# Causal mask as a matmul, and the copies of keys and queries spread anew over the engines

## The chip, the cores and the metric

One core of one Trainium2 chip runs the whole kernel as one program. The metric is device time in microseconds (us) of one execution; lower is better. The engines are named as the profile names them: PE (TensorE, matmuls; PEld is its weight load), DVE (VectorE), ACT (ScalarE), POOL (GpSimd), SP (SyncE, which here only issues DMAs). Each engine works through its own queue in order; an instruction at the head of a queue that waits holds all behind it.

## The reference, cut to what matters

Inputs are q, k, v of shape (4 batches, 8 heads, 768 positions, 64) and the weights of a mixture of experts. First comes an attention in which each query sees only the 6 best of its causal key chunks (32 keys each), then a dense two-layer network plus one of 8 experts per token.

```python
k_min, k_max = k_chunks.min(axis=3), k_chunks.max(axis=3)          # per chunk of 32 keys
ub = sum(maximum(q * k_min, q * k_max))                            # bound of a query on a chunk
ub = where(causal_chunk, ub, -1e9); top_chunks = argsort(ub)[..., -6:]
mask = (chunk of the key in top_chunks) & (pos_q >= pos_k)
attn = softmax(where(mask, scale * q @ k.T, -1e9)); out = attn @ v
x = out as (3072 tokens, 512)
y = relu(x @ w1_dense) @ w2_dense + gate * (relu(x @ w1[e]) @ w2[e])   # e = argmax of x @ w_gate
```

## The kernel before, in words

**Tiles.** The 32 (batch, head) pairs are taken two heads at a time: 16 pairs p, four per batch. One pair has 768 positions, six tiles of 128. Inside a tile of 128 queries or keys the positions are permuted (two interleaved halves of 64), which is why the causal pattern of a diagonal block is written with two nested steps.

**Operands of the score matmul.** For head g of a pair, `kT[i][g]` (stationary) and `rT[i][g]` (moving) are 128 x 768 arrays in f16. For head 0, rows 0 to 63 hold the 64 coordinates of the keys (negated queries in `rT`) and rows 64 to 95 hold `exf`, a matrix of 30000 where a key belongs to a chunk (in `rT`: flags, 1 where a query does not select the chunk). For head 1 it is the other way round: chunk rows at 0, coordinates at 64. So one matmul gives minus the score plus 30000 for every key that was not selected, and `exp(-0.125 * ...)` is then the softmax numerator. There are NB = 3 buffers i, used by pairs p, p+3, and so on.

**Preparation of a pair** is done two pairs ahead:

- `cast_qk`, `cast_v` (L464 to L476): GpSimd casts the loaded f32 tiles to f16 `k16`, `q16`, `v16`.
- `prep_k` (L478): six PE transposes into PSUM `pk`; ACT copies them to SBUF `kp` (L484); DVE takes maximum and minimum over each chunk into `ks` (L495, two instructions); DVE multiplies by a head mask into `kb` (L498).
- `prep_q` (L505): six transposes into PSUM `pq`; ACT writes `qp`, the relu of it (L513); DVE writes `rT[i][0]`, the negated whole (L514), and `rT[i][1][64:128]`, the negated lower half (L515).
- `prep_kt` (L500): DVE copies the two halves of `kp` into `kT[i][0]` and `kT[i][1]` (L502, L503).
- `prep_ub` (L517): the chunk bounds, 19 small matmuls on `qp`, `rT` and `kb` (L521, L525), ten DVE max8 (L531) and the DVE comparison that makes the flags `fl` (L533).
- `prep_s` (L535): transposes of the flags (L539) and two DVE copies into the chunk rows of `rT` (L541, L542).

**Units.** The block-triangle of scores of one pair is cut into 11 units of up to 512 columns. `scores(p, u)` (L544) issues the matmuls of a unit into one of three PSUM buffers `sp`, ACT takes the exponential into `ex` (L555), and for the three units per pair that consist of four diagonal blocks GpSimd zeroes the future keys in `ex` with an affine_select (L557). `av(p, u)` (L561) multiplies `ex` by the values (L570); `norm` divides by the row sums.

**Order.** A hand-written sequence runs over (p, u): scores two units ahead, `av` one unit behind; `prep_s` of p+1 at u = 2, `prep_k`, `prep_q`, `prep_kt`, `prep_ub` of p+2 at u = 4, 5, 7, 9; casts at u = 0 and u = 7, tied by `issue_after(latest["pool"])` behind the last GpSimd instruction recorded there; the weights of one or two expert layers are loaded by GpSimd-issued DMAs at u = 0 (L206). Between the units of pairs 4 to 15 stand "fills": the transposes, gate, dense layers (L257, L265, L385, L387, L394, L397) and the scatter of tokens into the table (L370) of the batch that was finished before. A list scheduler draws up each engine's final order from priorities and estimated times, so an engine's order need not be that of the source.

**After the attention** come 28 expert blocks (L688 to L733) with the rest of the last batch's dense work, on PE nearly without a gap.

Of the kernel before, what the change touches and what calls it, by code (L numbers as in the profile page):

```python
# [10 lines left out]
HF = mybir.dt.float16  # L11
AF = mybir.ActivationFunctionType
ALU = mybir.AluOpType
# [4 lines left out]
def kernel(  # L18
# [12 lines left out]
    nc = tc.nc  # L31
    B, H, S, D = q.shape
    NT = S // 128
    NC = S // 32
# [30 lines left out]
    NJ = 2  # L65
# [10 lines left out]
    acst = att.enter_context(tc.tile_pool(name="acst", bufs=1))  # L76
# [54 lines left out]
                                fill=-60000.0, base=j, pattern=[[128, NT], [0, 2], [-32, NC]], channel_multiplier=2)  # L131
    for i in range(NB):
        nc.vector.memset(kT[i][0][64:128], 0.0)
        nc.vector.memset(kT[i][1][0:64], 0.0)
        nc.vector.memset(v16[i][:, :, :, D : D + 1], 1.0)

    def members():
# [2 lines left out]
        nc.gpsimd.affine_select(out=exf[0:32], in_=exf[0:32], compare_op=ALU.is_ge, fill=0.0,  # L140
                                base=31, pattern=[[-1, S]], channel_multiplier=32)

    def expand(i):
        nc.scalar.copy(kT[i][0][64:96, :], exf[0:32])
        nc.scalar.copy(kT[i][1][0:32, :], exf[0:32])


    iom8 = const.tile([128, NT, E], FP)
# [308 lines left out]
    with (  # L457
# [20 lines left out]
        def prep_k(p):  # L478
            s = st[p]
            pk = pprep.tile([128, S], HF, name="pk", tag="pp")  # L480
            for t in range(NT):
                nc.tensor.transpose(pk[:, t * 128 : (t + 1) * 128], s["k16"][:, t].rearrange("p g d -> p (g d)"), ident)  # L482
            s["kp"] = kp = ahead.tile([128, S], HF, name="kp")
            nc.scalar.copy(kp.rearrange("d (T p j) -> d T p j", p=128, j=NJ),  # L484
                           pk.rearrange("d (T j p) -> d T p j", p=128, j=NJ))
            ks = ahead.tile([128, 2, NC], HF, name="ks")
            if p == 0:

                pc = pk.rearrange("d (T j c w) -> d T c j w", j=NJ, c=8, w=16)
                for i, op in enumerate((ALU.max, ALU.min)):  # L490
                    nc.vector.tensor_reduce(out=ks[:, i].rearrange("d (T c) -> d T c", c=8), in_=pc, op=op,
                                            axis=mybir.AxisListType.XY)
            else:
                for i, op in enumerate((ALU.max, ALU.min)):
                    nc.vector.tensor_reduce(out=ks[:, i], in_=kp.rearrange("d (c w) -> d c w", w=32), op=op,  # L495
                                            axis=mybir.AxisListType.X)
            s["kb"] = kb = ahead.tile([128, 2, 2, NC], HF, name="kb")
            nc.vector.tensor_tensor(kb, ks.unsqueeze(2).to_broadcast([128, 2, 2, NC]), hmask, ALU.mult)  # L498

        def prep_kt(p):  # L500
            kp = st[p]["kp"]
            nc.vector.tensor_copy(kT[p % NB][0][0:64], kp[0:64])  # L502
            nc.vector.tensor_copy(kT[p % NB][1][64:128], kp[64:128])  # L503

        def prep_q(p):  # L505
            s = st[p]
            pq = pprep.tile([128, S], HF, name="pq", tag="pp")
            pqv = pq.rearrange("d (T h j p) -> d T h j p", h=2, j=NJ, p=64)
            for t in range(NT):
                nc.tensor.transpose(pqv[:, t // NJ, :, t % NJ], s["q16"][:, t].rearrange("p g d -> p (g d)"), ident)  # L510
            s["qp"] = qp = ahead.tile([128, S], HF, name="qp")
            r0, r1 = rT[p % NB]
            nc.scalar.activation(qp, pq, AF.Relu)  # L513
            nc.vector.tensor_single_scalar(r0, pq, -1.0, ALU.mult)  # L514
            nc.vector.tensor_single_scalar(r1[64:128], pq[64:128], -1.0, ALU.mult)  # L515

        def prep_ub(p):  # L517

# [2 lines left out]
            nc.tensor.matmul(ub.rearrange("p t g c -> p (t g c)"), ident, cbias.rearrange("p t g c -> p (t g c)"),  # L521
                             start=True, stop=False, skip_group_check=True)
            for t in range(NT):
                for n, (src, j) in enumerate(((s["qp"], 0), (s["qp"], 1), (rT[p % NB][0], 1))):
                    nc.tensor.matmul(ub[:, t].rearrange("p g c -> p (g c)"), src[:, t * 128 : (t + 1) * 128],  # L525
                                     s["kb"][:, j].rearrange("p g c -> p (g c)"),
                                     start=False, stop=(n == 2), skip_group_check=True)
# [16 lines left out]
        def scores(p, u):  # L544
            s = st[p]
            pc = units[u]
            sp = psc.tile([128, 512], FP, name="sp")
            o = 0
            for g, kt, a, z in pc:
                w = (z - a) * 128  # L550
                nc.tensor.matmul(sp[:, o : o + w], kT[p % NB][g][:, kt * 128 : (kt + 1) * 128],  # L551
                                 rT[p % NB][g][:, a * 128 : z * 128], start=(o == 0), stop=True, skip_group_check=True)
                o += w
            ex = aexp.tile([128, 512], HF, name="ex")
            nc.scalar.activation(ex[:, 0:o], sp[:, 0:o], AF.Exp, scale=-0.125)  # L555
            if pc[0][1] == pc[0][2]:
                latest["pool"] = nc.gpsimd.affine_select(out=ex, in_=ex, compare_op=ALU.is_ge, fill=0.0, base=0,  # L557
                                        pattern=[[0, 4], [1, 2], [2, 64]], channel_multiplier=-1)
            s["ex", u] = ex

        def av(p, u):  # L561
# [260 lines left out]
```

## Time and profile before

| | us |
|---|---|
| median of 3 runs (lowest, highest) | 259.67 (257.14, 260.58) |
| the profiled execution | 257.31 |
| its span in the profile | 255.5 |
| busy: PE, DVE, ACT, POOL | 213.7, 179.3, 176.1, 159.6 |

The span runs from the first to the last instruction of the program; the 1.8 us between it and the execution's own time lie around it. A busy PE in the records is not a PE at its peak: a matmul's record holds a fixed start-up time beside its streaming time, and matmuls that follow each other overlap in it. Rows of groups read: line, engine, operation, tiles, shape, count, then busy time in us (overlaps counted once), mean ns of one, then the engine's idle time just before and what ended it.

### The profile page before, as it was taken

The numbers are of one execution on the slowest core, as the hardware profiler recorded it, in microseconds if no ns is written. First come the engines' busy times: TensorE is split into PE (matmuls) and PEld (weight loads), VectorE is DVE, ScalarE is ACT, GpSimd is POOL, SyncE is SP. The second block draws the span as 40 slices with busy tenths as digits, with TensorE's granted clock in tenths as the row PEclk, the third lists the DMA queues.
The fourth block names the chain that finished last, engine by engine and source line by source line (L and its number), as shares of the span: only waits on it lengthen the run. The fifth ranks groups of instructions, "written<-read, shape, count | busy, mean of one in ns | idle before, by whom it ended". The sixth has DMA issues, their size and how long they took to land.

```text
span 255.5 us, 7236 instructions
## 1 busy us (share of the span) xinstructions
PE 213.7 (84%) x2547; PEld 141.8 (55%) x2547; DVE 179.3 (70%) x558; ACT 176.1 (69%) x332; POOL 159.6 (62%) x198
## 2 busy tenths in 40 slices
PE   0378969888989899999988988889769999999970
PEld 0256746656657576766567755555335554555530
DVE  6869989999979689998898895167223345555540
ACT  2799979878779898878889778815356555455440
POOL 4746998566276987168986145514744463887881
PEclk9999999999999999999999999999999999999997
DMA  6999999999999799989999924447879999787885
GB/s 172 262 267 228 217 227 239 220 232 202 239 174 292 132 276 226 250 179 242 298 230 258 190 72 128 144 114 218 234 154 208 220 209 200 124 140 97 117 112 105
DMA packets 75124, 50.12 MB, mean 196 GB/s; under 512 B 29648, under 2 KB 68176, under 8 KB 75088
## 3 DMA queue, kind: packets, MB, share of 16 engines
q1 hardware_dynamic: 59856, 30.33, 46.9%
q0 software_dynamic: 15232, 19.32, 45.6%
q8 instruction: 21, 0.34, 0.6%
q14 instruction: 15, 0.12, 0.1%
HBM read 41.93 MB, written 18.23 MB: 235 GB/s over the span
## 4 chain that ended last, share of the span: by engine, by line
PE 29%; DVE 22%; POOL 18%; issue 10%; DMA 7%; ACT 6%; SPq 3%; another core or an unknown queue 1%; POOLq 0%; DVEq 0%; ACTq 0%
DVE ks L495 7%; POOL out_dram L733 7%; PE hp L696 6%; PE yp L725 6%; PE hp L385 4%; POOL ex L557 3%; PE yp L394 3%; POOL table L370 2%; SPq L92 2%; DMA vf<-in_v_dram 2%; ACT ex L555 2%; ACT kp L484 2%; DVE kT L503 2%; DMA kf<-in_k_dram 2%; PE sp L551 2%
## 5 line engine op out<-in xcount | busy, mean ns | idle before, releaser
L555 ACT ACTIVATE ex<-sp 128x512 f16<-128x512 f32 (+1 forms) x176 | 90.9, 608 | 8.9 <-PE sp L551 4.6
L551 PE MATMUL sp<-rT,kT 128*128 128x128 f16 (+3 forms) x384 | 64.4, 260 | 4.0 <-ACT ex L555 2.7
L733 POOL DMA_INDIRECT out_dram<-yo,xg x28 | 43.3, 1545 | 23.5 <-DVE yo L732 9.8
L557 POOL TENSOR_SCALAR_AFFINE_SELECT ex<-ex 128x512 f16<-128x512 f16 x48 | 32.6, 694 | 36.9 <-ACT ex L555 30.8
L570 PE MATMUL op<-v,ex 128*128 128x65 f16 x672 | 48.4, 194 | 3.3 <-POOL ex L557 1.8
L570 PEld LDWEIGHTS <-ex 128*128 128x128 f16 x672 | 36.9, 98 | 19.0 <-POOL ex L557 6.4
L370 POOL DMA_INDIRECT table<-xbig,slot x24 | 23.9, 997 | 20.2 <-issue 15.1
L732 DVE TENSOR_SCALAR yo<-yp,xg 128x512 f32<-128x512 f32 x27 | 20.3, 751 | 22.2 <-PE yp L725 13.3
L551 PEld LDWEIGHTS <-kT 128*128 128x128 f16 x384 | 29.0, 98 | 7.7 <-issue 4.2
L725 PE MATMUL yp<-we,ehT 128*128 x112 | 28.7, 379 | 3.9 <-ACT ys L397 2.5
L707 ACT COPY ehT<-tp 128x512 f16<-128x512 f16 x28 | 16.4, 585 | 21.5 <-PE tp L705 16.7
L696 PE MATMUL hp<-we,exT 128*128 x112 | 29.1, 379 | 2.0 <-DMA xg<-table 1.2
L495 DVE TENSOR_REDUCE ks<-kp 128x24 f16<-128x768 f16 x30 | 27.3, 943 | 4.2 <-ACT kp L484 3.9
L385 PE MATMUL hp<-xT,wd 128*128 128x384 f16 x128 | 26.2, 325 | 0.8 <-DVE xT L258 0.8
L699 ACT ACTIVATE eh<-hp 128x512 f16<-128x512 f32 x28 | 16.7, 597 | 11.4 <-PE hp L696 10.1
L394 PE MATMUL yp<-wd,hT 128*128 128x512 f16 x96 | 23.9, 379 | 0.3 <-issue 0.3
L690 DVE COPY exT<-tp 128x512 f16<-128x512 f16 x28 | 11.8, 423 | 17.4 <-PE tp L688 9.9
L387 ACT ACTIVATE hT<-hp 128x384 f16<-128x384 f32 x32 | 16.1, 505 | 9.0 <-PE hp L385 6.2
L397 ACT COPY ys<-yp 128x512 f32<-128x512 f32 x24 | 14.3, 598 | 9.5 <-PE yp L394 4.3
L484 ACT COPY kp<-pk 128x768 f16<-128x768 f16 x16 | 12.9, 806 | 8.8 <-PE pk L482 8.8
L581 DVE TENSOR_TENSOR xbig<-op,rs 128x384 f16<-128x384 f32 x32 | 17.5, 547 | 0.2
L725 PEld LDWEIGHTS <-ehT 128*128 128x128 f16 x112 | 10.1, 98 | 12.6 <-issue 2.8
(127 smaller groups left out, 383.1 us busy)
## 6 DMA issues: line engine op xcount, KB each, us to landing
we<-in_moe_w_dram POOLq DMA_DIRECT2D x16, 512.0 KB
kf<-in_k_dram SPq DMA_DIRECT2D x32, 192.0 KB
qf<-in_q_dram SPq DMA_DIRECT2D x32, 192.0 KB
vf<-in_v_dram SPq DMA_DIRECT2D x32, 192.0 KB
out_dram<-ys SPq DMA_DIRECT2D x48, 128.0 KB
xg<-table SPq DMA_DIRECT2D x28, 136.0 KB
table<-zt SPq DMA_DIRECT2D x9, 136.0 KB
wd<-in_moe_w_dense_dram POOLq DMA_DIRECT2D x2, 512.0 KB
```

The costliest lines, as they stand in the source:

```text
L370: sc = nc.gpsimd.indirect_dma_start(out=table, out_offset=bass.IndirectOffsetOnAxis(ap=keep["slot"][:, t : t + 1], axis=0), in_=xbig[b % 2 ...
L385: nc.tensor.matmul(hp, wd[:, ko, j * 128 : (j + 1) * 128], xT[:, ko, g * G * 128 : (g + 1) * G * 128], start=(ko == 0), stop=(ko == NK - 1))
L394: nc.tensor.matmul(yp, hold["h"][:, j, i * 128 : (i + 1) * 128], wd[:, NK + j], start=(j == 0), stop=(j == NK - 1))
L495: nc.vector.tensor_reduce(out=ks[:, i], in_=kp.rearrange("d (c w) -> d c w", w=32), op=op, axis=mybir.AxisListType.X)
L551: nc.tensor.matmul(sp[:, o : o + w], kT[p % NB][g][:, kt * 128 : (kt + 1) * 128], rT[p % NB][g][:, a * 128 : z * 128], start=(o == 0), sto ...
L555: nc.scalar.activation(ex[:, 0:o], sp[:, 0:o], AF.Exp, scale=-0.125)
L557: latest["pool"] = nc.gpsimd.affine_select(out=ex, in_=ex, compare_op=ALU.is_ge, fill=0.0, base=0, pattern=[[0, 4], [1, 2], [2, 64]], chan ...
L570: nc.tensor.matmul(s["op", g][:, t * (D + 1) : (t + 1) * (D + 1)], ex[:, o : o + 128], v16[p % NB][:, g, kt, :], start=first, stop=(last_o ...
L696: nc.tensor.matmul(hp, s["xT"][:, ko], wef[:, bass.ds(offs[i] + ko * 512, 512)], start=(ko == 0), stop=(ko == NK - 1))
L725: nc.tensor.matmul(yp, s["hT"][:, j], wef[:, bass.ds(offs[i] + (NK + j) * 512, 512)], start=(j == 0), stop=(j == NK - 1))
L732: nc.vector.tensor_scalar(o, yp, gate, None, ALU.mult)
L733: sc = nc.gpsimd.indirect_dma_start(out=out, out_offset=to, in_=o, in_offset=None, bounds_check=N - 1, oob_is_err=False, compute_op=ALU.by ...
```

## The change

Five edits, all in the attention:

1. **Mask.** The affine_select on `ex` (48 of them) goes. A constant 128 x 128 matrix `later` with 30000 where the key lies after the query is made once; a diagonal unit starts with a matmul of the identity with `later` (repeated four times, 512 columns) into `sp`, and the score matmuls accumulate on top.
2. **Keys leave PSUM once.** ACT writes all 128 rows straight into `kT[i][1]`; the separate `kp` tile goes. GpSimd then copies rows 0 to 63 into `kT[i][0]` and overwrites rows 0 to 31 of `kT[i][1]` with `exf`. This last copy is made for every pair now, where `expand` made it once per buffer on ACT.
3. **Negated queries leave PSUM once.** DVE writes the negated whole into `rT[i][1]`; GpSimd copies rows 0 to 63 into `rT[i][0]`.
4. **Relu** of the queries goes from ACT to DVE, read from PSUM.
5. **`kb`**, the product of chunk bounds and head mask, goes from DVE to GpSimd.

For pair 0, edits 2 to 5 keep DVE and ACT in place of GpSimd. `latest["pool"]`, behind which the casts and scatters are tied, is now set by the copies of `prep_q` and `prep_kt`.

```diff
+    later = acst.tile([128, 128], HF)
+    nc.vector.memset(later, 0.0)
+    nc.gpsimd.affine_select(out=later, in_=later, compare_op=ALU.is_ge, fill=30000.0, base=0,
+                            pattern=[[1, NJ], [NJ, 64]], channel_multiplier=-1)
     def expand(i):
         nc.scalar.copy(kT[i][0][64:96, :], exf[0:32])
-        nc.scalar.copy(kT[i][1][0:32, :], exf[0:32])
...
-            s["kp"] = kp = ahead.tile([128, S], HF, name="kp")
+            kp = kT[p % NB][1]
...
-            nc.vector.tensor_tensor(kb, ks.unsqueeze(2).to_broadcast([128, 2, 2, NC]), hmask, ALU.mult)
+            (nc.gpsimd if p else nc.vector).tensor_tensor(kb, ks.unsqueeze(2).to_broadcast([128, 2, 2, NC]), hmask, ALU.mult)
 
         def prep_kt(p):
-            kp = st[p]["kp"]
-            nc.vector.tensor_copy(kT[p % NB][0][0:64], kp[0:64])
-            nc.vector.tensor_copy(kT[p % NB][1][64:128], kp[64:128])
+            k0, k1 = kT[p % NB]
+            if p:
+                nc.gpsimd.tensor_copy(k0[0:64], k1[0:64])
+                latest["pool"] = nc.gpsimd.tensor_copy(k1[0:32], exf[0:32])
+            else:
+                nc.vector.tensor_copy(k0[0:64], k1[0:64])
+                nc.scalar.copy(k1[0:32], exf[0:32])
...
-            nc.scalar.activation(qp, pq, AF.Relu)
-            nc.vector.tensor_single_scalar(r0, pq, -1.0, ALU.mult)
-            nc.vector.tensor_single_scalar(r1[64:128], pq[64:128], -1.0, ALU.mult)
+            if p:
+                nc.vector.tensor_single_scalar(r1, pq, -1.0, ALU.mult)
+                nc.vector.tensor_single_scalar(qp, pq, 0.0, ALU.max)
+                latest["pool"] = nc.gpsimd.tensor_copy(r0[0:64], r1[0:64])
+            else:
+                nc.scalar.activation(qp, pq, AF.Relu)
+                nc.vector.tensor_single_scalar(r1, pq, -1.0, ALU.mult)
+                nc.vector.tensor_single_scalar(r0[0:64], pq[0:64], -1.0, ALU.mult)
...
-                for n, (src, j) in enumerate(((s["qp"], 0), (s["qp"], 1), (rT[p % NB][0], 1))):
+                for n, (src, j) in enumerate(((s["qp"], 0), (s["qp"], 1), (rT[p % NB][1], 1))):
...
+            diag = pc[0][1] == pc[0][2]
+            if diag:
+                nc.tensor.matmul(sp.rearrange("p (n k) -> p n k", k=128), ident, later.unsqueeze(1).to_broadcast([128, 4, 128]),
+                                 start=True, stop=False, skip_group_check=True)
...
-                                 rT[p % NB][g][:, a * 128 : z * 128], start=(o == 0), stop=True, skip_group_check=True)
+                                 rT[p % NB][g][:, a * 128 : z * 128], start=(o == 0 and not diag), stop=True,
+                                 skip_group_check=True)
...
-            if pc[0][1] == pc[0][2]:
-                latest["pool"] = nc.gpsimd.affine_select(out=ex, in_=ex, compare_op=ALU.is_ge, fill=0.0, base=0,
-                                        pattern=[[0, 4], [1, 2], [2, 64]], channel_multiplier=-1)
```

(`diag` in the score unit means that every piece of it is a diagonal block. The memset of `kT[i][1][0:64]`, three at the start, goes too.)

More of the change, by code (lines that the diff above doesn't have):

```diff
@@ L133 @@
         nc.vector.memset(kT[i][0][64:128], 0.0)
-        nc.vector.memset(kT[i][1][0:64], 0.0)
         nc.vector.memset(v16[i][:, :, :, D : D + 1], 1.0)
```

## The prediction

> **What bounds the kernel now.** I read the page's totals first, then the engines' busy time cut by stage, then the chain that ended last for each stage, then the waits.
>
> ```profile
> span 255.5 us, 7236 instructions
> PE 213.7 (84%) x2547; PEld 141.8 (55%) x2547; DVE 179.3 (70%) x558; ACT 176.1 (69%) x332; POOL 159.6 (62%) x198
> ```
>
> Over the whole span no engine is full. The averages mix an attention that the change touches with an expert phase that it doesn't, so they decide nothing. The table by stage has cuts at the first exponential, at the start of pair 5 (where the dense fills begin in earnest), and at the last exponential; the last row is a piece of the expert phase.
>
> ```profile
> core 0: us, PE busy (x) PEld busy (x) DVE busy (x) ACT busy (x) POOL busy (x), PEclk, DMA share, GB/s
> 0.00:17.18 17.18, 6.08 (x56) 4.80 (x57) 12.24 (x41) 9.95 (x12) 9.78 (x18) 1.00 1.00 235
> 17.18:55.12 37.94, 31.09 (x503) 22.65 (x503) 35.49 (x117) 32.29 (x64) 28.97 (x52) 1.00 1.13 223
> 55.12:165.83 110.71, 100.71 (x1426) 72.48 (x1424) 92.20 (x314) 93.43 (x186) 69.69 (x92) 1.00 0.95 209
> 165.83:255.47 89.64, 75.79 (x564) 41.83 (x564) 39.42 (x88) 40.47 (x72) 51.14 (x36) 0.98 0.81 161
> 200.00:220.00 20.00, 19.57 (x139) 10.53 (x138) 8.72 (x16) 10.73 (x19) 10.46 (x7) 1.00 0.94 191
> ```
>
> Each row gives the stretch, its length, and per engine the busy time. The first stage is the start. The **light stage** (17.18 to 55.12, pairs 0 to 4, 7.6 us a pair) is led by DVE, 35.49 of 37.94 (94%), with ACT at 85% and PE at 82%. The **heavy stage** (110.71 us, some eleven pairs with fills) is led by PE, 100.71 (91%), with DVE at 83% and ACT at 84%. The expert phase is PE's: in the last row PE is busy 19.57 of 20.00 us, 98%. That row tells what PE reaches when nothing else is in the way. The clock column is 1.00 through the attention, so no time is lost there to a lower clock.
>
> ```profile
> by line: DMA vf<-in_v_dram 14.6%; POOL ex L557 11.6%; issue 9.6%; DVE ks L495 9.1%; POOL v L476 6.3%; DVE m L531 4.8%; POOL k L469 4.1%; POOL q L471 4.0%; DVE kT L503 4.0%; PE ps L539 3.6%; DVE rT L541 3.0%; DVE rT L515 3.0%; DVE rT L542 2.
> POOL ex L557 <- ACT ex L555: 30.8, 19, 6.2
> PEld L570 <- POOL ex L557: 6.4, 14, 1.4
> PEld L539 <- DVE fl L533: 4.8, 5, 1.4
> PE sp L551 <- ACT ex L555: 2.7, 6, 0.9
> PEld L510 <- DVE rT L542: 2.4, 2, 1.2
> PE ub L525 <- DVE kb L498: 0.8, 2, 0.6
> ```
>
> The first line is the chain in the light stage, by line; the others are waits in the attention (who waited for whom: us in total, times, longest). The chain passes through GpSimd's mask (11.6%) and through its casts of v, k and q (6.3, 4.1, 4.0%), although no PE instruction needs those casts soon: they are on it because the mask stands behind them in the same queue. And the queue stands still in turn, 30.8 us in 19 times, until an exponential is there to be masked. So GpSimd, 63% busy in the heavy stage, couples casts, scatters and the score pipeline. The other members are DVE's: `ks`, the copies into `kT`, the negation L515. No wait here is PE's own making.
>
> **The change part by part.** Durations from the groups (busy us, mean ns of one):
>
> ```profile
> L557 POOL TENSOR_SCALAR_AFFINE_SELECT ex<-ex 128x512 f16<-128x512 f16 x48 | 32.6, 694 | 36.9 <-ACT ex L555 30.8 <-DMA kf<-in_k_dram 5.4 <-issue 0.4
> L394 PE MATMUL yp<-wd,hT 128*128 128x512 f16 x96 | 23.9, 379 | 0.3 <-issue 0.3
> 110.45 1.89 PE yp L394 x8
> L502 DVE COPY kT<-kp 64x768 f16<-64x768 f16 x16 | 7.0, 437 | 0.1
> L503 DVE COPY kT<-kp 64x768 f16<-64x768 f16 x16 | 8.0, 500 | 0.3
> L498 DVE TENSOR_TENSOR kb<-ks,hmask 128x96 f16<-128x96 f16 x16 | 5.7, 357 | 0.0
> L515 DVE TENSOR_SCALAR rT<-pq 64x768 f16<-64x768 f16 x16 | 9.0, 561 | 0.5
> L514 DVE TENSOR_SCALAR rT<-pq 128x768 f16<-128x768 f16 x16 | 8.7, 546 | 0.0
> L513 ACT ACTIVATE qp<-pq 128x768 f16<-128x768 f16 x16 | 13.3, 829 | 0.5 <-PE pq L510 0.5
> L471 POOL CAST q<-qf 128x768 f16<-128x768 f32 x16 | 13.3, 832 | 1.4 <-DMA qf<-in_q_dram 0.9 <-PE pk L482 0.5
> L138 POOL TENSOR_SCALAR_AFFINE_SELECT exf<-exf 32x768 f16<-32x768 f16 x1 | 0.8, 815 | 0.0
> L364 POOL COPY xbig<-num 128x6 int32<-128x6 int32 x4 | 0.7, 185 | 0.0
> ```
>
> *PE.* 48 matmuls of 512 columns are added, three a pair. One alone takes 0.379 us; eight in a row take 1.89, so each further one costs (1.89 - 0.379) / 7 = 0.216 and 0.163 is start-up that overlaps when PE is fed. I take 0.216 (a mask matmul is always followed by four score matmuls): 48 x 0.216 = 10.4 us, 3.2 in the light stage (15 of them) and 7.1 in the heavy one (33). Alone it would be 18.2; below 0.216 nothing speaks for it.
>
> *DVE.* Each pair from 1 on loses 0.437 + 0.500 (key copies) + 0.357 (`kb`) + 0.561 (second negation) and gains a relu from PSUM, priced as L514, the same source, shape and kind: 0.546. Net -1.31 us a pair.
>
> *ACT.* The relu goes: -0.83 a pair. Three of six copies of `exf` at the start go, one comes.
>
> *GpSimd.* Three masks go: -2.08 us a pair. Three copies of 768 columns and `kb` come. No row has an f16 copy of this size on GpSimd: the cast over 768 columns (0.832) and the 32-partition select over 768 (0.815) agree, so 0.83; the low end is DVE's 0.437 for the same copy. `kb`, 96 elements from two inputs, lies between the 6-element copy (0.185) and the 512-column select (0.694); I take 0.40, nearer to the short one. Sum 3 x 0.83 + 0.40 = 2.89, net +0.81 a pair (-0.58 at the low ends, +1.1 at the high ones). What hides it: these operands are for two pairs on, and no exponential waits in this queue any more. Queued behind the new copies are the casts of pairs p+2 and p+3, the weight loads and the scatters, none needed within a pair's time; only `kb` is needed soon.
>
> **Light stage.** New busy times over five pairs: DVE 35.49 - 5 x 1.31 = 28.9; ACT 32.29 - 5 x 0.83 = 28.1; GpSimd 28.97 - 15 x 0.694 + 5 x 2.89 = 33.0; PE 31.09 + 3.2 = 34.3. PE leads, and at the 98% of the expert phase the stage takes 34.3 / 0.98 = 35.0: **-2.9 us**. GpSimd at 33.0 is close behind; it too would have to keep busy.
>
> **Heavy stage.** PE becomes 100.71 + 7.1 = 107.8, DVE 92.2 - 11 x 1.31 = 77.8, ACT 84.3, GpSimd 69.7 + 11 x 0.81 = 78.6. With the others at three quarters and less, PE should come near 98% again: 110.0. Besides, each wait that vanishes lets a matmul overlap its 0.163 us of start-up; the PE and PEld rows above count 14 + 5 + 6 + 2 + 2 = 29 such waits in the attention. I take nine of them for the heavy stage, 1.5 us: 108.5, **-2.2 us**. This is the weakest term. Bounds: 117.8 (all idle stays and the matmuls come on top, +7.1) and 103.1 (no idle, and all 29 start-ups overlapped: 107.8 - 4.7, -7.6).
>
> **Start.** The first exponential follows this run on ACT:
>
> ```profile
> 15.79 0.79 ACT L542 COPY rT<-ps 64x768 f16<-64x768 f16 x1
> 16.48 0.81 ACT L513 ACTIVATE qp<-pq 128x768 f16<-128x768 f16 x1
> 17.18 2.04 ACT L555 ACTIVATE ex<-sp 128x512 f16<-128x512 f32 x4
> 11.76 0.36 DVE L503 COPY kT<-kp 64x768 f16<-64x768 f16 x1
> 12.13 0.91 DVE L531 MAX8 m<-ub 128x8 f32<-128x8 f32 x10
> ```
>
> The relu of pair 1 leaves ACT (17.18 - 16.48 = 0.70) and one key copy leaves DVE before the first max8 (0.36): **-1.1 us**. The constant `later` is made while GpSimd waits for its first load; it costs nothing, and some 0.5 us if that load were there.
>
> **Sum:** -2.9 - 2.2 - 1.1 = -6.2 us against the profiled execution's 257.31 (span 255.5 and 1.8 around it), 251.1. That execution is close to the lowest of the runs (257.14); the median of the runs is 259.67, and on that scale the forecast is 253.5, 2.4% faster. A change within 2%, 5.2 us, is about what this kernel's measurement can't tell from none.
>
> **The rivals.**
>
> *The mask matmuls eat the gain.* PE leads the heavy stage already, and work that was on a 63% busy engine is put onto it. If half of PE's idle there stays (5.0 us), the stage takes 107.8 + 5.0 = 112.8, +2.1, and the total is -1.9: 257.8. For it: the dependence inside a pair (bounds, max8, flags, transposes; the 4.8 us row of L539) is a latency and doesn't shrink with load. Against: DVE's queue, in which these steps stand, loses 1.31 us a pair. If all idle stays: +7.1 - 4.0 = +3.1, 262.8, still within 2%. A variant with GpSimd as the bound of the light stage (33.0 busy, but not gapless) ends in the same place.
>
> *`kb` comes late (slower).* `kb` gates the bounds matmuls L525, which stand in PE's queue with all later scores behind them. PE already waits for it here (0.8 us, twice). On GpSimd the product can stand behind two casts (2 x 0.83) and takes 0.40: 1.2 us late beyond the slack would cost 14 pairs x 1.2 = 16.8, less 6.2: +10.6, 270. It decides from (5.2 + 6.2) / 14 = 0.81 us a pair. Against: the bounds come five units after the transposes of the keys, and the scheduler orders by estimated times. [...]
>
> ```profile
> L498 DVE TENSOR_TENSOR kb<-ks,hmask x16: 193/251/741, 9.7 to 149.0; 128x96 f16<-128x96 f16 x16
> L502 DVE COPY kT<-kp x16: 310/352/794, 11.0 to 150.4; 64x768 f16<-64x768 f16 x16
> ```
>
> These (least, median, longest ns) show that DVE's SBUF instructions are at times held to twice their median and more while GpSimd works. With them gone from DVE, there is nothing left in the preparation of pairs 1 to 15 to be held so, or to hold `kb`; I lower this rival's chance for it, from 0.16 to 0.13, and give the 0.03 to the rival before. [...]
>
> *More is released than I count.* The masks and GpSimd's casts together are 26% of the light stage's chain; if the heavy stage gets to its lower bound, 103.1, the total is -2.9 - 7.6 - 1.1 = -11.6: 248.1.
>
> **How the numbers follow.** Forecast 0.42 (own range 250 to 255); released more 0.06; gain eaten 0.36; `kb` late 0.13; other slower cases (an order of the scheduler that puts casts too late) 0.03. Faster by over 2%: 0.42 + 0.06 = 0.48; within: 0.36; slower: 0.16. The range leaves out the slower cases, 0.16, and next to nothing else: 247 to 263 takes in 248.1 and 262.8, the two ends of the heavy stage's bounds.
>
> **What would show it.** Right: no waits of L570 on GpSimd; PE at 97% or more in both attention stages, with 0.22 us of added streaming per mask matmul; the last exponential near 159.5; the copies at 0.83. Wrong: PE idle before L525 for `kb` (rival two); PE's idle share in the heavy stage still near 9% (rival one); GpSimd at 95% in the light stage with casts on the chain; a first exponential later than 17.2, if the casts of pair 2 stand behind the copies of pair 1.

## The result and the profile after

The changed kernel takes 261.52 us (median of 20 runs, 259.6 to 267.2), the kernel before, run beside it, 257.81 (20 runs, 256.37 to 264.79). The ratio is 1.0122, interval 1.009 to 1.0155: 1.2% slower, where 2.4% faster was forecast. The change's own profiled execution (263.93 us, span 262.2) is one of its slower ones, with a mean granted clock of 0.969, so the lines below are mostly those of a later execution of the same kernel on another chip (255.37 us, span 253.7, clock 0.982, called `changed_again`).

The totals and the table by stage of `changed_again`, cut as before at the first exponential, the start of pair 5 and the last exponential:

```profile
span 253.7 us, 7288 instructions
PE 220.0 (87%) x2595; PEld 147.1 (58%) x2595; DVE 162.0 (64%) x510; ACT 166.2 (66%) x315; POOL 167.5 (66%) x211
```

```profile
core 0: us, PE busy (x) PEld busy (x) DVE busy (x) ACT busy (x) POOL busy (x), PEclk, DMA share, GB/s
...
16.06:53.04 36.98, 34.54 (x533) 25.69 (x531) 30.86 (x105) 30.97 (x61) 30.38 (x55) 1.00 1.07 212
53.04:168.10 115.06, 104.10 (x1445) 74.83 (x1443) 82.38 (x282) 87.27 (x175) 76.84 (x102) 0.99 0.96 209
168.10:253.65 85.55, 75.14 (x564) 41.88 (x564) 39.34 (x88) 40.60 (x71) 50.11 (x35) 0.97 0.82 169
```

The start is 1.12 us shorter (17.18 to 16.06), the light stage 0.96 (37.94 to 36.98), and the heavy stage is 4.35 longer (110.71 to 115.06). In the change's own execution it is longer still:

```profile
53.08:170.16 117.08, 106.69 (x1445) 76.03 (x1443) 82.50 (x282) 86.59 (x175) 76.94 (x102) 0.97 0.97 213
```

The expert phase, which the change doesn't touch, was 89.64 us before, 92.05 in this execution and 85.55 in `changed_again`. Over all profiles of this study it lies between 84.6 and 93.7, whatever was done to the attention. So a single total says little here, and I compare the lengths of the attention stages beside the ratios. The profiles come from several chips, and the kernel before, as it is, was profiled on one of them only, so a difference of a stage by 1 or 2 us between chips is weak evidence.

Where does the heavy stage's time go? PE is busy 3.4 us longer (100.71 to 104.10) and idle 1.0 longer (10.0 to 10.96). The groups of PE's instructions in the heavy stage alone, with the idle time before them in the last column, say that it isn't the old idle time. `changed_again`:

```profile
L538 PE MATMUL ub<-kb,qp 128*128 128x48 f16 x120 | 5.9, 183 | 3.7 <-POOL kb L501 3.7
...
L552 PE MATMUL ps<-ident,fl 128*128 128x128 f16 x60 | 5.0, 219 | 2.7 <-DVE fl L546 2.4 <-issue 0.2
L485 PE MATMUL pk<-ident,k 128*128 128x128 f16 x54 | 4.8, 228 | 4.1 <-DVE mxv L271 3.8
```

The kernel before:

```profile
L570 PE MATMUL op<-v,ex 128*128 128x65 f16 x466 | 34.7, 194 | 1.3 <-POOL ex L557 0.6 <-DVE xbig L581 0.4 <-ACT ex L555 0.2
...
L539 PE MATMUL ps<-ident,fl 128*128 128x128 f16 x60 | 5.0, 220 | 2.2 <-DVE fl L533 1.6 <-DVE m L531 0.6
L510 PE MATMUL pq<-ident,q 128*128 128x128 f16 x60 | 5.0, 219 | 1.8 <-DVE rT L542 1.8
```

Before, many small waits. After, three places hold 9.9 of the 10.96 us: the bounds matmuls wait 3.7 us for `kb`, now GpSimd's; one flag transpose waits 2.4; and the transposes of keys (L485) wait 3.8 for DVE's queue, at whose head the clearing of `dr`, which belongs to the expert phase, waits for a cast on GpSimd. That cast had itself waited 5.16 us for the load of its values. In the change's own execution the first two waits are there as well (3.5 us for `kb`, 2.4 for the flags); the third is not, `dr` waits 0.11 us, and PE stands 2.4 us in pair 14 instead. GpSimd's own wait for the exponentials (30.8 us in 19 times) exists no more.

The second and third come from one DVE instruction each, shown here in order of time (start, duration, engine), with the cast that held the second:

```profile
66.47 3.42 DVE L310 TENSOR_TENSOR osum<-osum 128x8 f16<-128x8 f16 x1
...
142.93 0.83 POOL L479 CAST v<-vf 128x768 f16<-128x768 f32 x1 [5.16 <-DMA vf<-in_v_dram]
143.93 0.48 DVE L730 MEMSET dr<- 128x512 f32 x1 [4.38 <-POOL v L479]
```

```profile
L310 DVE TENSOR_TENSOR osum<-osum x3: 161/163/3421, 66.5 to 146.9; 128x8 f16<-128x8 f16 x3
```

```profile
L307 DVE TENSOR_TENSOR osum<-osum x3: 153/164/164, 71.2 to 150.2; 128x8 f16<-128x8 f16 x3
```

The addition of counts (8 elements, two operands in SBUF; L307 before, the last row, L310 after) takes 0.16 us, and once 3.42. GpSimd's queue at that time, and what PE then waited for:

```profile
65.84 0.81 POOL L508 COPY kT<-exf 32x768 f16<-32x768 f16 x1
66.61 0.82 POOL L524 COPY rT<-rT 64x768 f16<-64x768 f16 x1
67.38 0.82 POOL L472 CAST k<-kf 128x768 f16<-128x768 f32 x1
68.15 0.82 POOL L474 CAST q<-qf 128x768 f16<-128x768 f32 x1
68.92 0.18 POOL L367 COPY xbig<-num 128x6 int32<-128x6 int32 x1
69.06 0.82 POOL L479 CAST v<-vf 128x768 f16<-128x768 f32 x1
```

```profile
71.96 0.51 PE L552 MATMUL ps<-ident,fl 128*128 128x128 f16 x6 [2.41 <-DVE fl L546]
```

GpSimd runs the new copies and the casts without a pause, and the addition ends as the run does. Behind it in DVE's queue stand `norm`, the max8 and the flags, and PE stands still for them. In the change's own execution the same addition took 3.42 us too.

The prices of the single instructions, by groups:

```profile
L564 PE MATMUL sp<-later,ident 128*128 128x512 f16 x48 | 18.3, 382 | 6.1 <-POOL later L144 5.9
...
L524 POOL COPY rT<-rT 64x768 f16<-64x768 f16 x15 | 12.4, 828 | 0.8 <-DVE rT L522 0.8
...
L523 DVE TENSOR_SCALAR qp<-pq 128x768 f16<-128x768 f16 x15 | 8.2, 546 | 0.0
L501 POOL TENSOR_TENSOR kb<-ks,hmask 128x96 f16<-128x96 f16 x15 | 5.5, 368 | 7.4 <-DVE ks L498 7.3
```

### The profile page after: what moved, and what is told of

It is laid out like the page before. It is cut to its first block, busy times and chain, and to the rows that moved or that the text cites. A ratio compares the mean times of both kernels' runs of the same rounds, so it can differ in the third digit from the quotient of the medians.

```text
span 262.2 us, 7288 instructions
## 1 busy us (share of the span) xinstructions
PE 226.5 (86%) x2595; PEld 149.2 (57%) x2595; DVE 162.3 (62%) x510; ACT 165.5 (63%) x315; POOL 167.7 (64%) x211
## 4 chain that ended last, share of the span: by engine, by line
PE 47%; DMA 9%; POOL 7%; issue 6%; DVE 5%; ACT 4%; SPq 0%; POOLq 0%; DVEq 0%; ACTq 0%
PE hp L711 9%; PE yp L740 8%; PE hp L388 6%; PE sp L568 5%; PE yp L397 5%; DMA vf<-in_v_dram 4%; DMA table<-xbig,slot 3%; POOL out_dram L748 3%; PE op L585 3%; PE tp L703 2%; PE tp L720 2%; DMA out_dram<-ys 2%; ACT ex L573 2%; PE tp L260 1%; ACT kT L487 1%
## 5 line engine op out<-in xcount | busy, mean ns | idle before, releaser
L585 PE MATMUL op<-v,ex 128*128 128x65 f16 x672 | 51.0, 195 | 1.8 <-issue 0.9
L585 PEld LDWEIGHTS <-ex 128*128 128x128 f16 x672 | 39.2, 99 | 16.5 <-issue 2.5
L373 POOL DMA_INDIRECT table<-xbig,slot x24 | 24.1, 1005 | 29.1 <-issue 21.1
L568 PEld LDWEIGHTS <-kT 128*128 128x128 f16 x384 | 30.6, 99 | 9.6 <-issue 2.6
L722 ACT COPY ehT<-tp 128x512 f16<-128x512 f16 x28 | 16.4, 585 | 23.9 <-PE tp L720 17.7
L388 PE MATMUL hp<-xT,wd 128*128 128x384 f16 x128 | 27.6, 338 | 1.7 <-issue 1.5
L498 DVE TENSOR_REDUCE ks<-kT 128x24 f16<-128x768 f16 x30 | 27.1, 943 | 2.6 <-ACT kT L487 2.3
L397 PE MATMUL yp<-wd,hT 128*128 128x512 f16 x96 | 25.9, 400 | 0.0
L507 POOL COPY kT<-kT 64x768 f16<-64x768 f16 x15 | 12.3, 823 | 19.1 <-ACT kT L487 19.1
L564 PE MATMUL sp<-later,ident 128*128 128x512 f16 x48 | 18.3, 382 | 6.1 <-POOL later L144 5.9
L487 ACT COPY kT<-pk 128x768 f16<-128x768 f16 x16 | 12.8, 803 | 11.3 <-PE pk L485 7.6
L544 DVE MAX8 m<-ub 128x8 f32<-128x8 f32 (+4 forms) x160 | 15.1, 164 | 7.1 <-PE ub L538 7.0
```

Source lines behind the costliest of these rows:

```text
L373: sc = nc.gpsimd.indirect_dma_start(out=table, out_offset=bass.IndirectOffsetOnAxis(ap=keep["slot"][:, t : t + 1], axis=0), in_=xbig[b % 2 ...
L388: nc.tensor.matmul(hp, wd[:, ko, j * 128 : (j + 1) * 128], xT[:, ko, g * G * 128 : (g + 1) * G * 128], start=(ko == 0), stop=(ko == NK - 1))
L397: nc.tensor.matmul(yp, hold["h"][:, j, i * 128 : (i + 1) * 128], wd[:, NK + j], start=(j == 0), stop=(j == NK - 1))
L564: nc.tensor.matmul(sp.rearrange("p (n k) -> p n k", k=128), ident, later.unsqueeze(1).to_broadcast([128, 4, 128]), start=True, stop=False, ...
L585: nc.tensor.matmul(s["op", g][:, t * (D + 1) : (t + 1) * (D + 1)], ex[:, o : o + 128], v16[p % NB][:, g, kt, :], start=first, stop=(last_o ...
```

## The experiments

My theory after the result: the loss is three new waits, `kb` late on GpSimd, DVE's SBUF instructions held by GpSimd's unbroken runs (the addition for 3.42 us where it takes 0.16), and `dr`. The rivals: PE's streaming of the mask matmuls is the price; and transfers set the pace, so that whatever is saved is waited for elsewhere. Ratios are to the kernel before, run on the same chip in the same series; series stood on different chips, so ratios are compared within one. The length of a pair is the time from its first exponential to that of the next pair.

**First series: the parts.** The changed kernel once more:

> The changed kernel once more, for a profile that is not disturbed. PE theory (the 48 mask matmuls stream 10.4 us on the engine that leads the heavy stage, and too little is bought back): heavy stage 112 to 115 us against 110.7 before, PE busy about 107, its waits short and many. GpSimd theory (the copies put on GpSimd hold VectorE and delay the product of bounds and head mask): a VectorE instruction of 8 elements held for some 3 us again, and PE waiting for it and for the product, 4 us or more in the heavy stage. Total 260 to 262 by both.

258.03 us, ratio 1.0112 (1.0042 to 1.0183): the loss is there on this chip too.

The mask back on GpSimd, all the rest of the change kept (the mask matmul goes, `later` with it):

```diff
-            if diag:
-                nc.tensor.matmul(sp..., ident, later...)
             nc.scalar.activation(ex[:, 0:o], sp[:, 0:o], AF.Exp, scale=-0.125)
+            if pc[0][1] == pc[0][2]:
+                latest["pool"] = nc.gpsimd.affine_select(out=ex, in_=ex, ...)
```

> The change without its first edit: the mask is the affine_select on GpSimd again, all else as changed. PE theory: PE loses 10.4 us, 7.1 of them in the heavy stage: 252 to 255, faster than before and than the change. GpSimd theory: GpSimd now has masks and copies, 8.8 us of work a pair, and the masks stand behind the copies: 263 or more.

270.52 us, ratio 1.0585 (1.0505 to 1.0665). GpSimd is then busy 40.37 of the light stage's 46.42 us and holds it up (the matmuls that need the masked `ex` wait 5.4 us for it; the granted clock was 0.85 in the mean of the stage): it can't carry masks and copies. The matmul is the smaller evil.

The kernel before with edit 1 alone (casts and scatters are tied behind the cast of the values, as there is no mask to tie them to):

```diff
+            if diag:
+                nc.tensor.matmul(sp..., ident, later...)
-            if pc[0][1] == pc[0][2]:
-                latest["pool"] = nc.gpsimd.affine_select(out=ex, in_=ex, ...)
...
-                st[p]["cast"] = nc.gpsimd.tensor_copy(v16..., st[p]["v"])
+                latest["pool"] = st[p]["cast"] = nc.gpsimd.tensor_copy(v16..., st[p]["v"])
```

> The kernel before with the first edit alone: mask by matmul, all copies, relu and the product where they were. The scatters and casts are tied behind the last cast of values, since no mask is left on GpSimd. PE theory: +3 to +6 us on before, 261 to 264. GpSimd theory: GpSimd is relieved by 33 us and holds nobody: 257 or less.

257.99 us, ratio 1.011 (1.0036 to 1.0184), as slow as the whole change. Its stages and its `kb`, which here is still DVE's (least, median, longest ns):

```profile
17.47:57.01 39.54, 33.68 (x518) 24.75 (x518) 38.44 (x117) 32.81 (x65) 19.46 (x37) 1.00 1.14 223
57.01:168.92 111.91, 105.67 (x1458) 75.13 (x1456) 89.25 (x314) 93.76 (x186) 48.50 (x60) 1.00 0.95 205
```

```profile
L503 DVE TENSOR_TENSOR kb<-ks,hmask x15: 189/201/1772, 18.5 to 152.1; 128x96 f16<-128x96 f16 x15
...
  PE ub L530: 3.2, 4
```

GpSimd is half idle now (19.46 of 39.54), and yet DVE is fuller: 38.44, 97%, against 94% before. The longest `kb` grew from 0.741 us to 1.772, and PE's waits for it from 0.8 to 3.2. The two longest products (1.77 and 1.76 us) stood beside a cast of k and a cast of q, one right behind the other, and ended with the second. In the kernel before, two products met such a pair of casts and ended with the first (0.74 and 0.49 us). My reading is that the waiting masks had cut GpSimd's work in pieces and so let DVE in; what lets it in between two casts is not shown.

The count addition takes 0.16 us here each time, and `dr` waits 1.74 us. So the first edit alone, with `kb` still on DVE and without the held addition, already loses as much as the five together.

The mask matmul issued twice per diagonal unit:

```diff
-            if diag:
+            for rep in range(2 if diag else 0):
                 nc.tensor.matmul(sp..., ident, later..., start=(rep == 0), ...)
```

> The changed kernel with the mask matmul issued twice in each diagonal unit (48 more matmuls of 512 columns; the masked scores then carry 60000 in place of 30000). PE theory: each of the 33 in the heavy stage costs its 0.216 us in full, those of the light stage part of it: 7 to 10 us on the change, 268 to 271. GpSimd theory: PE has room, 0 to 4 us.

256.56 us, ratio 1.0008 (0.9953 to 1.0064): 48 more matmuls, and no loss that can be measured.

```profile
16.06:53.73 37.67, 36.28 (x555) 27.07 (x554) 33.34 (x106) 31.07 (x61) 31.33 (x56) 1.00 1.06 207
53.73:173.14 119.41, 110.08 (x1472) 77.44 (x1468) 78.11 (x280) 88.79 (x175) 76.13 (x101) 0.97 0.95 207
```

The profiled execution's attention is 5.0 us longer than `changed_again`'s, but with a longer wait of PE behind `dr` (5.26 us, against 3.82) and a longer stretch at half clock (6.8 against 3.4). PE's busy time rises by 1.74 + 5.98 = 7.7 us for 48 matmuls, 0.16 each with the longer half clock in it, less than the 0.216 that I took. The rival of the streaming is weakened, as doubling it does not double the loss, but not ruled out: the order of DVE's queue came out another way here, and the count addition took 0.16 us at 62.99, so this kernel has no hold to pay for.

**Second series: the three waits one by one, and together.** `dr` cleared behind the expert phase's first copy of `xT`:

```diff
-            nc.vector.memset(dr, 0.0)
+            with tc.issue_after(latest["xT"].ins):
+                nc.vector.memset(dr, 0.0)
```

> The changed kernel, with the memset of the expert phase's tile dr tied behind a copy of the expert phase, so that it stands late in VectorE's queue. Memset theory (in the changed kernel the scheduler put it ahead of the flag copies of pair 15, and it waits there for the last cast of values and so for its load: VectorE stood 4.4 us, PE 3.8): the stall goes, 3 to 4 us less than the change: ratio to before 0.995 to 1.00. Product theory (PE's waits for the product on GpSimd, 4.0 us in the heavy stage, are the loss): no gain, ratio 1.01.

262.16 us, ratio 1.0156 (1.0092 to 1.0221). The wait for `dr` is gone, and nothing is won: the heavy stage takes 116.23, with pair 14 now at 14.2 us where `changed_again` had 9.2 (more on that at `best_of`). There may have been nothing to win: in `count_on_gpsimd`, of the same series, the clearing stands at its old place and waits 0.12 us.

`kb` back on DVE:

```diff
-            (nc.gpsimd if p else nc.vector).tensor_tensor(kb, ks..., hmask, ALU.mult)
+            nc.vector.tensor_tensor(kb, ks..., hmask, ALU.mult)
```

> The changed kernel with the product of bounds and head mask on VectorE, as before. Product theory: PE's waits for it fall from 4.0 to about 1 us, 3 us less than the change: ratio 1.00. Memset theory: the stall of the memset stays, ratio 1.01.

293.0 us, ratio 1.1345 (1.1281 to 1.1409). This miss told the most.

```profile
L501 DVE TENSOR_TENSOR kb<-ks,hmask x15: 628/2932/3778, 18.0 to 176.2; 128x96 f16<-128x96 f16 x15
...
  PE ub L538: 13.6, 8
```

```profile
36.58 2.93 DVE L501 TENSOR_TENSOR kb<-ks,hmask 128x96 f16<-128x96 f16 x1
```

```profile
36.32 0.82 POOL L508 COPY kT<-exf 32x768 f16<-32x768 f16 x1 [0.20 <-DVE ks L498]
37.10 0.82 POOL L472 CAST k<-kf 128x768 f16<-128x768 f32 x1
37.87 0.82 POOL L474 CAST q<-qf 128x768 f16<-128x768 f32 x1
38.64 0.82 POOL L479 CAST v<-vf 128x768 f16<-128x768 f32 x1
39.41 0.44 POOL L174 MEMSET xbig<- 128x192 f16 x2
```

A product that takes 0.20 us undisturbed (the median of the experiment above) takes 2.93 in the median. It starts 0.26 us into a GpSimd copy and ends at 39.51, when GpSimd has turned from copies to a memset. Of the 15 products ten ended like this, with the run of copies and casts that they met; five got in between two of them (0.73 to 2.27 us). The relu from PSUM just ahead of it in DVE's queue (L523, 36.12 to 36.66, beside a copy from 36.32 on) took 0.54 us, as always: it is not held. So edit 5, which I feared, is what keeps the change from losing 13%.

The count addition on GpSimd:

```diff
-  nc.vector.tensor_add(osum[:, b + 1], osum[:, b + 1], osum[:, b])
+  nc.gpsimd.tensor_add(osum[:, b + 1], osum[:, b + 1], osum[:, b])
```

> The changed kernel with the addition of token counts (8 elements, two inputs from SBUF) on GpSimd in place of VectorE. Port theory (that addition was held 3.3 us while GpSimd copied without a pause, and PE then stood 2.4 us): 2 to 4 us less than the change, ratio 0.995 to 1.00; no VectorE instruction is held for over 1 us. Else ratio 1.01.

260.46 us, ratio 1.0065 (1.0018 to 1.0112), the lowest of the series; the heavy stage falls to 113.97. PE no longer stands before L552 (0.2 us). The hold was worth some 2 us: the heavy stage is 2.3 shorter than that of `memset_late`, pair 6, where the hold was, falls from 15.1 to 12.4, and the ratio is 0.9% lower, though the two intervals overlap.

All three edits, `kb` on DVE included:

> The three edits together. If the three one-off waits are the whole of what took the forecast gain, their sum comes back: 8 to 10 us less than the change: ratio 0.97 to 0.98. If they hide one another or PE's streaming takes their place: 0.995 to 1.01.

290.96 us, ratio 1.1213 (1.1123 to 1.1302): the held `kb` swamps the rest.

**Third series: transfers, and `kb` elsewhere.** Half of each expert layer's weight load is left out in both kernels (that half is cleared at the start instead, which puts 5.5 to 6.6 us in front of the first exponential):

```diff
-  nc.gpsimd.dma_start(out=we[:, e, w * NK : (w + 1) * NK], ...)
+  nc.gpsimd.dma_start(out=we[:, e, w * NK : w * NK + 2], ...)
```

> The changed kernel with half of each expert weight matrix left out of the load (two of four row blocks; the rest is set to zero by VectorE ahead of everything, which makes the start some 8 us later, so that stages are compared and not totals). This takes 8 MB of reads out of the attention. DMA theory (the transfers of the attention, some 33 MB by 150 us in every kernel so far, are what the change runs into: the last load of values and the stores of dense rows come late): the heavy stage falls from 114 to 116 us to below 108, the last pairs lose their stalls, and the changed kernel is then 4 us or more ahead of the kernel before with the same weights left out. Engine theory (PE's streaming and its waits for the product): heavy stage within 2 us of what it was.

> The kernel before with the same half of the expert weights left out of the load. DMA theory: it gains less than the changed kernel, 0 to 3 us in the heavy stage, as DVE, ACT and the masks on GpSimd pace it. Engine theory: the same as the changed kernel gains, near nothing.

Ratios 1.0183 (1.0104 to 1.0262) and 1.0344 (1.0253 to 1.0435). Of the two heavy stages, the changed kernel's is the first row, that of the kernel before the second:

```profile
59.18:169.57 110.39, 103.94 (x1445) 74.84 (x1443) 82.24 (x282) 87.10 (x175) 76.46 (x102) 0.98 0.77 182
```

```profile
61.84:170.58 108.74, 101.37 (x1426) 72.62 (x1424) 92.52 (x314) 92.70 (x186) 68.95 (x92) 1.00 0.71 170
```

Against `changed_again` the changed kernel's heavy stage loses 4.7 us (115.06 to 110.39), that of the kernel before 2.0 (110.71 to 108.74). But pair 13 alone makes up more than the 4.7: it takes 11.5 us in place of 16.6, as `dr` waits 0.12 us here; and with all weights loaded it takes 11.4 or 11.5 too in the change's own execution, `memset_late` and `count_on_gpsimd`. Side by side, with fewer transfers, the changed kernel's stage is still 1.6 us the longer one, and the 108 of the DMA theory is not reached. A share of the transfers in the loss is neither shown nor excluded: the late load behind `dr` in `changed_again` was one. That the changed kernel comes out ahead here (medians 260.38 and 263.22) lies in the start, with the first exponential at 21.60 against 23.81, and not in the attention.

Weight loads two per pair in pairs 2 to 5 rather than 10 to 13, with the count addition on GpSimd:

```diff
-                for _ in range(2 if p >= 10 else 1):
+                for _ in range(2 if p <= 5 else 1):
```

> The changed kernel with the token counts added on GpSimd, and the two-a-pair weight loads moved from pairs 10 to 13 to pairs 2 to 5. DMA theory: the late load of values and the late stores between 138 and 155 us go, 3 to 5 us, part of which comes back in the light stage, whose DMA share is over 1 already: ratio 0.99 to 1.00. Engine theory: no change, 1.005 to 1.01.

256.68 us, between 251.44 and 260.19 in four runs, too wide for a ratio: inconclusive. The heavy stage, 113.48, is that of `count_on_gpsimd` within 0.5, though not in the same places: pair 6 takes 18.3 us against 12.4 (PE waits 3.1 for `kb` there, and 6.8 run at half clock), pair 14 9.5 against 13.4.

`kb` by four small ScalarE copies (halves of `ks`, the second with the sign turned, into buffers whose other halves stay zero), and the count addition on GpSimd:

```diff
+  for i in range(2):
+      nc.scalar.activation(kb[64:128, i, 0], ks[64:128, i], AF.Copy, scale=1.0 - 2 * i)
+      nc.scalar.activation(kb[0:64, i, 1], ks[0:64, i], AF.Copy, scale=1.0 - 2 * i)
```

> [...] Product theory: PE's waits for it, 4 to 5.5 us, fall below 1.5: ratio 0.99. DMA theory: the pace is set elsewhere, 1.005.

257.94 us, ratio 1.0076 (1.0008 to 1.0145).

```profile
16.13:54.50 38.37, 36.03 (x534) 26.77 (x532) 30.93 (x105) 34.52 (x81) 29.11 (x50) 1.00 1.02 204
54.50:164.05 109.55, 103.92 (x1445) 74.53 (x1443) 79.08 (x279) 94.21 (x215) 74.09 (x95) 1.00 1.01 219
```

In the profiled execution (250.84 us, the lowest of ten) PE is busy 95% of a heavy stage of 109.55, 4.4 less than `count_on_gpsimd`'s 113.97, and PE's wait before these matmuls falls from 5.1 us to 1.7 in the stage. But the 4.4 are not the price of `kb` on GpSimd: pair 14 alone is 4.6 shorter (8.8 us against 13.4), and the other ten pairs of the stage take about as long together as there (100.8 and 100.5). ACT, which now makes the product, is busy 8.1 us more in the stage. The light stage pays 1.3, as ACT is busy 34.52 us there, where it was 30.98. The attention as a whole, 147.9 us, is below the 148.65 of the kernel before on another chip. But the ten runs lie between 250.84 and 260.66, their median 7 us above this execution, so the total settles nothing.

**Fourth series: all repairs together.** `best_of` has the count addition on GpSimd, `kb` on ScalarE, `dr` late, and `later` made behind pair 0's casts; `best_of_early` has the weight loads of `weights_early` on top; the third is the kernel before with the count addition on GpSimd:

> The changed kernel with four repairs: the count addition (8 elements) on GpSimd, kb of pairs 1 to 15 by four small ScalarE copies, the clearing of dr tied behind the expert phase's first copy of xT, and the constant later made behind pair 0's casts. Theory (the loss is made of three new waits in the attention: kb on GpSimd, the held count addition, dr at the head of DVE's queue): the first exponential comes at 15.4 to 15.9 us (16.06 before this repair), heavy stage 108.5 to 110.5, so the attention ends 1 to 3 us sooner than that of the kernel before; ratio 0.985 to 0.998. Rival (the streaming of the 48 mask matmuls, 10.4 us, is what the kernel pays, and the repairs only move idle time about): heavy stage 112 or more, ratio 1.00 to 1.01. Rival (transfers set the pace: whatever is saved in the attention is given back to late loads): last exponential at 163 to 165 and still a ratio of 1.00 or more.

> best_of, with the second weight load per pair issued in pairs 2 to 5 rather than in pairs 10 to 13. Transfers theory: the expert weights are there sooner, so the stretch behind the last exponential shortens by 1 us or more against best_of, or its attention lengthens by as much as more traffic stands beside the loads of q, k and v. Theory of the new waits: same time as best_of within 1 us, as no wait of that theory is for these loads.

> The kernel before, with the count addition (8 elements) on GpSimd. If the hold of that addition needs an unbroken run of GpSimd copies, which the waiting masks broke up before, there is nothing to gain: ratio 0.997 to 1.006, heavy stage 110 to 112. If the addition was slow in the kernel before as well, a gain of 2 us or more in the heavy stage, ratio below 0.995.

264.67 us, ratio 1.0183 (1.0133 to 1.0233); 269.46 us, ratio 1.0395 (1.0342 to 1.0447); 259.71 us, ratio 0.9991 (0.9951 to 1.0032). The last says that the kernel before had nothing to gain: its addition was never held. The first falsifies my sum of repairs. Its table by stage, with five microseconds of pair 14 in the last row:

```profile
16.08:54.44 38.36, 35.68 (x534) 26.49 (x532) 30.92 (x105) 34.53 (x82) 29.19 (x51) 1.00 1.06 208
54.44:171.80 117.36, 106.39 (x1445) 75.57 (x1443) 79.00 (x278) 94.14 (x215) 74.22 (x95) 0.99 0.97 210
...
153.00:158.00 5.00, 1.02 (x10) 0.58 (x10) 0.73 (x3) 1.82 (x4) 2.50 (x3) 0.91 0.49 151
```

The light stage equals that of `product_on_scalar`, and so do pairs 5 and 6; pair 14 takes 14.7 us against 8.8. In it PE, DVE and ACT all stand, PE from 154.13 to 156.51 with nothing in the profile that it waits for, and two waits of the others are these:

```profile
DVE rs L599 <- remote: 4.7, 1, 4.7
ACT ex L578 <- remote: 3.1, 2, 2.2
```

"Remote" means that the records name no releaser. The same place took 13.9 us in the change's own execution, 14.2 in `memset_late` and 13.4 in `count_on_gpsimd`, but 9.2 in `changed_again` and 9.5 in `weights_early`: it came in the first measurement and in the second and fourth series, and not in the first and third. The kernel before has nothing like it (10.7, and 10.7 with the moved addition in the fourth series). GpSimd issues the scatter of a batch at that time (L373, 149.9 to 156.1 in `best_of`) and SyncE the stores of `ys`; whether these cause it was not tried. The moved `kb` and the late `dr` do not prevent it. For `best_of_early` a cause is in the waits:

```profile
POOL v L479 <- DMA vf<-in_v_dram: 15.2, 6, 7.0
...
POOL q L474 <- DMA qf<-in_q_dram: 6.5, 5, 4.0
```

With the weights loaded earlier, the casts wait 15.2 us for the loads of v and 6.5 for those of q, where in `best_of` it is 2.9 and 0.8; PE then waits for the cast of q (2.27 us before 76.19).

Taken together, the heavy stages (pairs 5 to 15) differ in a few pairs, in us:

| profile | pairs 5 and 6 | pair 13 | pair 14 | the other seven | heavy stage |
|---|---|---|---|---|---|
| before | 24.5 | 10.6 | 10.7 | 65.0 | 110.71 |
| the change's own | 25.7 | 11.5 | 13.9 | 66.1 | 117.08 |
| `changed_again` | 24.2 | 16.6 | 9.2 | 65.0 | 115.06 |
| `memset_late` | 24.2 | 11.4 | 14.2 | 66.5 | 116.23 |
| `count_on_gpsimd` | 21.6 | 11.5 | 13.4 | 67.5 | 113.97 |
| `product_on_scalar` | 23.9 | 12.4 | 8.8 | 64.5 | 109.55 |
| `best_of` | 23.9 | 12.5 | 14.7 | 66.3 | 117.36 |

In the seven other pairs the changed kernel is neither clearly faster nor clearly slower. Most of what makes its stage longer stands in pair 13 in one execution and in pair 14 in others.

No version of the study is faster than the kernel before by more than its interval.

## Why the prediction was wrong

**Start, -1.1: right.** 17.18 to 16.06 is -1.12; the relu and a key copy did leave the path. My "`later` costs nothing" holds at the end, though the trace shows it in front:

```profile
5.53 0.30 POOL L144 TENSOR_SCALAR_AFFINE_SELECT later<-later 128x128 f16<-128x128 f16 x1 [3.08 <-DVE later L143]
5.78 0.82 POOL L472 CAST k<-kf 128x768 f16<-128x768 f32 x1
```

```profile
4.96 0.82 POOL L469 CAST k<-kf 128x768 f16<-128x768 f32 x1 [2.51 <-DMA kf<-in_k_dram]
```

GpSimd waits for a memset of DVE, and the first cast starts 0.8 us later than before (last row). Made behind the casts in `best_of`, the first exponential came at 16.08, not sooner.

**Durations: right.** GpSimd's copies 0.83 (0.82 to 0.83 measured), `kb` 0.40 (0.37), the relu from PSUM 0.546 (0.546).

**Light stage, -2.9: mis-sized, -0.96.** PE's busy time was right (34.3, measured 34.54). The step that failed is "at the 98% of the expert phase": PE reached 93%. It stands idle 2.4 us there, 0.9 of them before the bounds matmuls, for `kb`, and 0.8 before the score matmuls; the rest is in smaller pieces. ACT's term was off too (30.97 busy, not 28.1).

**Heavy stage, -2.2: wrong in sign, +4.35.** The failed step is "with the others at three quarters and less, PE should come near 98% again": it was busy 90.5% of the stage, and 91.1% in the change's own execution, against 91% before. Shares of busy time say which engine could be the bound, not that nobody waits for an instruction that stands late in a queue. PE's busy time rose by 3.4 where I had 7.1, so the streaming was overpriced, and its idle time rose by 1.0 where I let it fall to 2.2. The old waits did vanish, as forecast. New ones of the same size took their place: 3.7 us for `kb`, 2.4 behind the held addition and 3.8 behind `dr` in `changed_again`, and in the change's own execution the first two and the stall in pair 14. The held addition was in no term of the sum; its removal gave back 2.7 us of pair 6.

**The rivals.** "All idle stays", 262.8, is near the measured 261.52, and its sign, an idle share of still 9% in the heavy stage, came true (9.5%). But its reason, a latency inside the pair that doesn't shrink, did not, and it had 7.1 us of streaming where PE's busy time rose by 3.4; that it came so near is luck. "`kb` comes late" had the place right and the price wrong: PE waits 4.6 us in 6 times in the attention, 0.33 us a pair, below the 0.81 from which it decides. Its move to ScalarE took 3.4 us from that wait in the heavy stage, but no time from the stage outside pair 14, so what the wait is worth is not shown.

**The argument that lowered that rival** is the clearest fault. I wrote that with DVE's SBUF copies gone there was nothing left in the preparation to be held, and put no price on a hold anywhere else. The count addition, outside the preparation, still read two operands from SBUF, and was held 3.42 us. And the spread that I quoted for `kb`, 193/251/741, was measured while the masks cut GpSimd's work in pieces; with the matmul mask it became 189/201/1772, and with the copies added 628/2932/3778. DVE's instruction mostly waited for the end of a run of GpSimd instructions (ten products of 15, and the held addition). For the rest of the preparation the argument agrees with the trace of the kernel before, where the negations from PSUM took 514 to 558 ns (L514, 16 times) and 560 to 563 (L515, 16), and the maximum and minimum of `kp` 912 to 954 (L495, 30): none of them was held there.

**What stays open:** the stall in pair 14 (no releaser in the records), why the first edit alone loses as much as all five, and the 84.6 to 93.7 us of the expert phase. Of the three waits only the held addition is shown by its removal, with some 2 us of the stage. A wait of 4 us or more before `dr` was met in the first series only, and the change lost in the first measurement without it. That the three make up the loss is not shown, since `best_of` is without them, but for 2.5 us before the bounds matmuls, and was slower.

## What to carry to other kernels

Before you move work to GpSimd, list the DVE instructions with two SBUF operands, however small (here eight elements took 3.42 us in place of 0.16), and ask what breaks up GpSimd's run of copies: a wait in its queue, which looks like waste, may be what lets DVE in (the longest `kb` took 0.74 us with the waiting masks and 1.77 without them). The idle share of the busiest engine was here made of single waits (three held 9.9 of 10.96 us); forecast it by asking who comes late in which queue, not by a utilisation that another stage reaches. And where an untouched stage varies by more than the forecast gain, as the expert phase does here (84.6 to 93.7 us), compare stage by stage.

## What the runs showed of the hardware

Beside GpSimd copies and casts back to back, two DVE instructions with two SBUF operands were held: in `product_on_vector` the product of 0.20 us took 2.93 (median of 15), and in `changed_again` and the change's own execution the addition of 0.16 once took 3.42, though it has only eight elements. Ten of the 15 products ended with the run, five got in between two GpSimd instructions (0.73 to 2.27 us). A DVE instruction from PSUM, beside a copy of such a run, took its usual 0.54.

Two rows show 3.4 us at a granted clock of 0.50 behind an idle stretch of PE. In `changed_again`, after the 3.8 us of idle PE behind `dr` (141.9 to 145.7):

```profile
145.50:148.90 3.40, 3.20 (x22) 2.26 (x23) 2.01 (x11) 1.53 (x3) 0.82 (x1) 0.50 1.08 174
```

In the change's own execution it came after 2.4 us of idle before 72.0 (row below), while in `changed_again` the same wait at the same place left the clock at 1.00 from 72.0 to 75.4. What decides this is not shown.

```profile
72.00:75.40 3.40, 3.40 (x24) 2.45 (x25) 1.11 (x2) 1.27 (x3) 1.93 (x3) 0.50 0.89 251
```
